# One more token tile through the DMA transpose, its plain load moved back, and a key stage opened with three tiles

## The chip, the cores and the metric

The kernel runs on one core of one Trainium2 chip. The metric is the time of one execution on the device, in microseconds (us). A profile of one execution gives its span from the first to the last instruction; the executions take some 2.0 to 2.1 us more than that. Runs are compared in rounds on the same chip, fast runs with fast runs. All results below are correct against the reference.

The engines' short names: PE is the TensorE matmul, PEld its weight load, DVE is VectorE, ACT is ScalarE, POOL is GpSimd, SP is SyncE. SP and ACT each issue loads on a hardware DMA queue of their own.

## The reference, cut to what matters

A linear-attention block and a token-mixing MLP share the input `x` (2048 tokens x 512, bf16) and are mixed by a gate. Only the keys matter here:

```python
qkv = (x @ wqkv)...                 # wqkv is 512 x 1536; the middle 512 columns give k
phi = lambda t: where(t > 0, t + 1, exp(t)) + 1e-6
pk  = phi(k)
kv  = einsum("bhsd,bhse->bhde", pk, v)   # the kernel uses x^T pk and multiplies by Wv afterwards
...                                 # normalizer, output projection, layernorm + MLP, gate
```

## The kernel before: the parts that the change and the argument touch

The tokens are cut into 16 tiles of 128. A tile's keys are four matmuls of 128x512, one for each quarter of `wk` (128 of the 512 inputs). They need the tile transposed (`xT`). Tiles 0 to 3 are loaded plainly into `xs` and transposed by TensorE with an identity; tiles 4 to 15 are transposed by DMA straight from DRAM and are loaded plainly as well, because the next matmul (`gacc`, which accumulates x^T pk) wants them untransposed.

The loads at the start, in the order in which they are issued on the queues of SP (`nc.sync`) and ACT (`nc.scalar`):

```python
load_x(nc.sync, 0, 1)
load_x(nc.scalar, 1, 1)
load_wk(nc.sync, 0)
load_x(nc.scalar, 2, 1)
load_x(nc.sync, 3, 1)
for k, q in ((1, nc.scalar), (2, nc.sync), (3, nc.scalar)):
    load_wk(q, k)
load_xT(4, 2)                 # DMA transpose of tiles 4 and 5, on SP
load_xT(6, 2)
load_x(nc.sync, 4, 4)
for t0, n in ((8, 4), (12, 4)):
    load_xT(t0, n)
    load_x(nc.sync, t0, n)
# ... wq, w1, wv, wo
```

The opening of the key stage:

```python
warm_up(6)                    # six matmuls on constants, for TensorE's clock
# ...
HEADS = 4
transpose_tile(0, False)      # four PE transposes and a copy on DVE (True: on ACT)
transpose_tile(1, True)
transpose_tile(2, False)
ln_step(0)
for k in range(2):            # first and second quarter of wk, tiles 0 to 2
    for t in range(HEADS - 1):
        k_part(t, (k,))
transpose_tile(HEADS - 1, True)
ln_step(1)
for t in range(HEADS):        # third and fourth quarter; all four for tile 3
    k_part(t, range(2 if t < HEADS - 1 else 0, ND))
    k_phi(t)
LAG = 4
for t in range(HEADS, NT):
    k_part(t, range(ND))
    k_phi(t)
    g_tile(t - LAG)           # gacc of tile t - 4
    # ... layernorm statistics of tile t - 3 on DVE
```

Below, "the first group" is the first-quarter matmuls of tiles 0 to 2, "the second group" their second-quarter matmuls, and "the third group" what begins with tile 0's third-quarter matmul.

The compiled program gives the hardware queues eight completion counters in turn. So the ninth DMA waits for the first to land before it is issued.

## Time and profile before

Before: 166.06 us (median of 3, from 165.96 to 166.17). The profiled execution:

| | |
|---|---|
| span | 164.0 us |
| PE busy | 158.9 us, 97% |
| chain that ended last | 95% PE |
| PE waits | 1.0 us in all, before 3.8 us |
| key stage (first key matmul to first `uacc`) | 5.01 to 33.14 us |

From the page of the kernel before: the span, and of part 1 busy time, share and number of instructions; of part 4 the shares of the chain of waits by engine.

```profile
span 164.0 us, 2057 instructions
PE 158.9 (97%) x771; PEld 74.1 (45%) x785; DVE 87.8 (54%) x200; ACT 58.7 (36%) x90; POOL 18.3 (11%) x37
PE 95%; DMA 2%; issue 1%; ACT 0%; DVE 0%
```

The kernel is bound by TensorE, so a few matmuls fewer ought to shorten it by their own length, as long as PE is not made to wait.

From the timeline of the kernel before, PE alone: start, length, engine, line, operation, tiles, shapes and count; in brackets how long the engine was idle before and what ended that.

```profile
2.93 0.63 PE L108 MATMUL wps<-const-bfloat16-1.0 128*128 128x512 bf16 x1
3.77 1.40 PE L194 MATMUL pt<-ident,xs 128*128 128x128 bf16 x12 [0.21 <-DMA xs<-in_A_x_dram]
5.01 1.74 PE L108 MATMUL kacc<-wk_sb,xT 128*128 128x512 bf16 x6
6.59 0.39 PE L194 MATMUL pt<-ident,xs 128*128 128x128 bf16 x4
6.81 2.11 PE L108 MATMUL kacc<-wk_sb,xT 128*128 128x512 bf16 x9
```

After the warm-up come the twelve transposes of tiles 0 to 2, the first and second group (six matmuls from 5.01 us), tile 3's four transposes (from 6.59 us) and the third group (from 6.81 us), which are the first of many matmuls without a gap. On PE the four transposes take the time from 6.59 to 6.81 us, which is 0.22 us.

From the timeline of SP's queue before (start and length of the issue, not of the transfer):

```profile
0.81 0.40 SPq L124 DMA_DIRECT2D xs<-in_A_x_dram  x1
1.27 0.43 SPq L127 DMA_DIRECT2D wk_sb<-in_A_wqkv_dram  x1
1.75 0.43 SPq L124 DMA_DIRECT2D xs<-in_A_x_dram  x1
2.23 0.44 SPq L127 DMA_DIRECT2D wk_sb<-in_A_wqkv_dram  x1
3.56 2.85 SPq L130 DMA_TRANSPOSE xT<-in_A_x_dram  x2
```

The first DMA transpose is the ninth DMA and goes out only at 3.56 us, when a completion counter is free.

### The profile page before, as it was taken

Reading aid. Unit: us, or ns where it says so; the run is one execution under the profiler, and the core shown is the slowest. Engines: PE = TensorE matmul, PEld = TensorE weight load, DVE = VectorE, ACT = ScalarE, POOL = GpSimd, SP = SyncE. Lnnn points to the kernel's source line nnn. Section 1 sums busy time; section 2 is a strip of 40 time slices with the busy share of each in tenths; the row PEclk is TensorE's granted clock in tenths of the full one; section 3 lists DMA queues with packets and bytes.
Section 4 is the critical chain, followed back from the end, with each engine's and each line's share of the span. In section 5 each row is a group of like instructions: output and inputs, shape, how many; then the busy total and the mean of one; then the engine's idle time right before and its main releaser. Section 6 shows DMA issues by size and latency. Waiting matters only on the chain.

```text
span 164.0 us, 2057 instructions
## 1 busy us (share of the span) xinstructions
PE 158.9 (97%) x771; PEld 74.1 (45%) x785; DVE 87.8 (54%) x200; ACT 58.7 (36%) x90; POOL 18.3 (11%) x37
## 2 busy tenths in 40 slices
PE   7999999999999999999999999999999999999992
PEld 2544444444544444434444444444444444444471
DVE  0599999958999999009994401256211111111131
ACT  3463386658577373212322113111122221111110
POOL 5000710200200000001055500050000000000000
PEclk9999999999999999999999999999999999999999
DMA  4999999999930005800993599932010011101001
GB/s 147 242 213 252 288 297 356 350 348 349 317 86 0 0 0 184 268 0 0 288 293 91 182 306 297 326 129 79 32 36 32 32 36 50 42 32 36 32 32 32
DMA packets 29993, 25.05 MB, mean 153 GB/s; under 512 B 7776, under 2 KB 29408, under 8 KB 29984
## 3 DMA queue, kind: packets, MB, share of 16 engines
q1 hardware_dynamic: 27968, 22.02, 45.0%
q0 software_dynamic: 1440, 2.38, 5.3%
q10 hardware_dynamic: 576, 0.52, 1.1%
q8 instruction: 6, 0.10, 0.3%
q14 instruction: 3, 0.02, 0.0%
HBM read 21.11 MB, written 2.23 MB: 142 GB/s over the span
## 4 chain that ended last, share of the span: by engine, by line
PE 95%; DMA 2%; issue 1%; ACT 0%; DVE 0%
PE uacc L108 29%; PE yps L108 29%; PE qacc L108 8%; PE gacc L108 8%; PE aps L108 8%; PE kacc L108 8%; DMA xs<-in_A_x_dram 2%; PE pt L194 1%; PE denps L108 1%; PE kvps L108 1%; PE wps L108 1%; ACT xT L198 0%; DVE ot L472 0%; PE zps L108 0%; PE pt L323 0%
## 5 line engine op out<-in xcount | busy, mean ns | idle before, releaser
L108 PE MATMUL uacc<-hs,w1c 128*128 128x512 bf16 x218 | 51.6, 379 | 0.4
L108 PE MATMUL yps<-uT,w2c 128*128 128x512 bf16 (+1 forms) x235 | 50.8, 366 | 0.2
L472 DVE SCALAR_TENSOR_TENSOR ot<-yps,c,a_sc 128x512 bf16<-128x512 f32 (+1 forms) x17 | 12.2, 719 | 46.1 <-PE yps L108 46.1
L108 PEld LDWEIGHTS <-w2c 128*128 128x128 bf16 x238 | 23.3, 98 | 25.3
L108 PEld LDWEIGHTS <-w1c 128*128 128x128 bf16 x224 | 21.6, 98 | 26.1 <-issue 0.4
L457 ACT ACTIVATE a_sc<-aps,c,gg 128x512 f32<-128x512 f32 x16 | 12.4, 778 | 46.7 <-PE aps L108 43.0
L317 ACT ACTIVATE uT<-uacc,bcol 128x512 bf16<-128x512 f32 x14 | 9.3, 687 | 27.7 <-PE uacc L108 27.7
L108 PE MATMUL qacc<-xT,wq_sb 128*128 128x512 bf16 x64 | 16.4, 379 | 0.0
L108 PE MATMUL aps<-W2sb,pqT 128*128 128x512 bf16 x62 | 16.2, 379 | 0.1
L108 PE MATMUL kacc<-wk_sb,xT 128*128 128x512 bf16 x63 | 15.9, 379 | 0.1
L108 PE MATMUL gacc<-pk,xs 128*128 128x512 bf16 x62 | 15.5, 379 | 0.1
L244 ACT ACTIVATE hs<-xs,nmr,rstd 128x512 bf16<-128x512 bf16 x16 | 12.8, 804 | 1.9 <-DVE nmr L238 1.9
L204 ACT ACTIVATE e<-qacc 128x512 bf16<-128x512 f32 x16 | 9.6, 597 | 10.1 <-PE qacc L108 10.1
L413 POOL DMA_DIRECT2D rex<-rd_dram x16 | 9.5, 603 | 23.0 <-DVE pqT L415 18.1
L204 ACT ACTIVATE e<-kacc 128x512 bf16<-128x512 f32 x16 | 9.3, 595 | 6.9 <-PE kacc L108 5.6
L208 DVE SCALAR_TENSOR_TENSOR pk<-kacc,e 128x512 bf16<-128x512 f32 x16 | 11.1, 692 | 0.6
L208 DVE SCALAR_TENSOR_TENSOR pqT<-qacc,e 128x512 bf16<-128x512 f32 x16 | 11.1, 692 | 0.6
L228 DVE BATCH_NORM_STATS2 stats<-xs 128x6 f32<-128x512 bf16 x16 | 10.9, 682 | 0.0
L205 DVE TENSOR_SCALAR e<-e 128x512 bf16<-128x512 bf16 x32 | 9.0, 281 | 3.1 <-ACT e L204 3.1
L400 DVE CUSTOM_DVE_ANT_0 junk<-xs,gw_b 128x512 bf16<-128x512 bf16 x16 | 9.8, 683 | 0.0
L108 PEld LDWEIGHTS <-xs 128*128 128x128 bf16 x64 | 6.3, 98 | 7.5
L108 PEld LDWEIGHTS <-pqT 128*128 128x128 bf16 x64 | 6.3, 98 | 7.6
(64 smaller groups left out, 73.2 us busy)
## 6 DMA issues: line engine op xcount, KB each, us to landing
w2c<-in_B_w_dram SPq DMA_DIRECT2D x4, 1792.0 KB, 8.8
w1c<-in_B_w_dram SPq DMA_DIRECT2D x2, 2048.0 KB, 15.5
w1c<-in_B_w_dram SPq DMA_DIRECT2D x3, 1024.0 KB, 12.3
rex<-rd_dram POOLq DMA_DIRECT2D x16, 128.0 KB, 2.9
out_dram<-ot SPq DMA_DIRECT2D x15, 128.0 KB, 1.7
xs<-in_A_x_dram SPq DMA_DIRECT2D x3, 512.0 KB, 5.3
wq_sb<-in_A_wqkv_dram SPq DMA_DIRECT2D x1, 512.0 KB, 6.9
wv_sb<-in_A_wqkv_dram SPq DMA_DIRECT2D x1, 512.0 KB, 10.9
```

The source lines that it names most:

```text
L108: nc.tensor.matmul(o, lhsT=lhsT, rhs=rhs, start=start, stop=stop, **kw)
L194: nc.tensor.transpose(pt[:, k * P : (k + 1) * P], xs[:, t, k * P : (k + 1) * P], ident[:])
L204: nc.scalar.activation(out=e[:], in_=acc[:], func=ACT.Exp)
L205: nc.vector.tensor_scalar(out=e[:], in0=e[:], scalar1=1.0, scalar2=PHI_EPS, op0=ALU.min, op1=ALU.add)
L208: nc.vector.scalar_tensor_tensor(out=dst, in0=acc[:], scalar=0.0, in1=e[:], op0=ALU.max, op1=ALU.add)
L228: nc.vector.bn_stats(out=stats[:], in_=xs[:, t, :])
L244: nc.scalar.activation(out=hs[:, t, :], in_=xs[:, t, :], func=ACT.Identity, scale=rstd[:, t : t + 1], bias=nmr[:, t : t + 1],)
L317: nc.scalar.activation(out=uT[:, j, :], in_=acc[:], func=ACT.Gelu_apprx_tanh, bias=bcol[:, j : j + 1])
L400: nc.vector.tensor_tensor_reduce(out=junk[:], in0=xs[:, t, :], in1=gw_b[:], scale=1.0, scalar=0.0, op0=ALU.mult, op1=ALU.add, accum_out=gp ...
L413: nc.gpsimd.dma_start(out=rex[:], in_=src.unsqueeze(1).to_broadcast([8, HEAD, SC]))
L457: nc.scalar.activation(out=a_sc[:], in_=aps[:], func=ACT.Identity, scale=gg[:, t : t + 1], bias=c2[:, t : t + 1],)
L472: nc.vector.scalar_tensor_tensor(out=ot[:, :W], in0=yps[:, :W], scalar=c1[:, t : t + 1], in1=a_sc[:, cs], op0=ALU.mult, op1=ALU.add,)
```

## The change

Its intent: save TensorE tile 3's four transposes and ACT their copy, by giving tile 3 to the DMA transpose as well; take tile 3's plain load from the crowded start, since it is then needed only by `gacc` and the statistics; and open the key stage with three tiles.

```diff
     load_x(nc.scalar, 2, 1)
-    load_x(nc.sync, 3, 1)
     for k, q in ((1, nc.scalar), (2, nc.sync), (3, nc.scalar)):
         load_wk(q, k)
-    load_xT(4, 2)
-    load_xT(6, 2)
-    load_x(nc.sync, 4, 4)
+    load_xT(3, 2)
+    load_xT(5, 3)
+    load_x(nc.sync, 3, 5)
 ...
-    HEADS = 4
+    HEADS = 3
     transpose_tile(0, False)
     transpose_tile(1, True)
     transpose_tile(2, False)
     ln_step(0)
+    ln_step(1)
     for k in range(2):
-        for t in range(HEADS - 1):
+        for t in range(HEADS):
             k_part(t, (k,))
-    transpose_tile(HEADS - 1, True)
-    ln_step(1)
     for t in range(HEADS):
-        k_part(t, range(2 if t < HEADS - 1 else 0, ND))
+        k_part(t, range(2, ND))
         k_phi(t)
 ...
-        g_tile(t - LAG)
+        if t >= LAG:
+            g_tile(t - LAG)
```

## The prediction

> **What bounds the kernel.** TensorE. The page gives PE 158.9 us of a 164.0 us span (97%); the chain that ended last is 95% PE; the view of waits lists 1.0 us for PE, all before 3.8 us. From 5.5 to 33.09 us, the end of the key stage, the chain is unbroken matmuls. DVE is nearly as full there (3.79 of 4 us in 20–24 us).
>
> **What the change removes.** Tile 3's four TensorE transposes. In the chain they stand at 6.75 us and cost 0.22 us (4 x 55 ns), all on the critical path. Also gone is a 0.60 us ACT copy at 7.01 us, off the path; DVE's phi work, which starts at 8.13 us, should move forward by about 0.2 us with the matmuls. The order of the rest hardly changes: tile 3's key matmuls come as one group of four at about 8.05 us; the first gacc group still follows tile 4.
>
> **What it adds and moves.** One more 128 KB tile through the DMA transpose: the two early transposes land about 7.66 and 8.55 us, 0.9 us apart for 256 KB, so a tile costs an estimated 0.45 us of DMA. Against that, a 128 KB load leaves the front of the SP queue, and the first transpose goes out sooner. Before, it was the ninth DMA of the two hardware queues; the program has eight completion counters, so it waited for the first load, 0.9 us on SP in the view of waits (issued at 3.56 us). Now it is the eighth and needs no wait: issue at about 2.2 us, landing (3.6 to 4.1 us on) at 6 to 7 us, needed at 8.05. Tiles 5–7: issue about 3.6, landing by about 9 us, needed at 10.65. Plain tile 3 (five-tile load, issue near 5.7, 5.3 us to land): about 11 us; needed by DVE's statistics near 13, by gacc near 15. Tiles 8–11 land no later than before (13.58), needed at 15.7. The w1 block lands at 26.7 against a need at 33.1. None should reach the chain.
>
> **The risk.** The transposes now run while the last two key weights are landing (before: issued 2.2 us, landing about 6.4–6.7 us); TensorE will want them at 6.75 and 6.97 us, 0.22 us sooner. The Trainium skill ("DMA: Bandwidth & Descriptors", section "Issuing engines are not separate DMA queues") says that all queues run on the same 16 engines and interleave. If the fourth quarter slips by over 0.3 us, PE stalls and the gain is eaten, at worst for some 0.5 us net loss. About one chance in five.
>
> **Predicted time.** 166.06 - 0.22 - a little = 165.8 us; 8 in 10: 165.4 to 166.3. Faster by over 2%: 0.01; within 2%: 0.98; slower by over 2%: 0.01.
>
> **What would show it.** Right: key matmuls contiguous from 5.5 us; key stage ends at about 32.87 us; every later stage as long as before; first DMA transpose issued near 2.2 us without a wait. Wrong: a PE wait on wk_sb or xT between 6.6 and 9 us, or on xs/pk near 13–15 us; a first transpose that still waits; DVE's last pk of the key stage (ends 31.81 us now) not moving forward, so that the last gacc group waits.
>
> **What would make it wrong.** The fourth key weight delayed by the transposes on the shared DMA engines; a transpose much slower beside plain loads; a shift of the first tile's landing, which would move the whole run.

## The result, and the profile after

The changed kernel took 166.31 us (median of 6, from 165.57 to 166.57); the kernel before, in the same rounds, 166.10 us (median of 6, from 165.96 to 166.50). The ratio is 1.0007, with a 95% interval from 0.9984 to 1.0029: the same. (Ratios here are the mean time of one kernel's fast runs over that of the other's of the same rounds, so not quite the ratio of the medians quoted.) The profiled execution took 166.53 us. All outputs are right.

From the page after, the lines of the span, of busy time, and of the chain:

```profile
span 164.3 us, 2060 instructions
PE 159.9 (97%) x781; PEld 74.0 (45%) x781; DVE 87.8 (53%) x200; ACT 58.2 (35%) x89; POOL 18.2 (11%) x37
PE 94%; DMA 3%; ACTq 1%; DVE 0%; issue 0%
```

PE's busy time is no measure of the saving. The trace of before holds ten matmul records fewer (771 against 781), although the program has four more, because some records are missing from a trace; and a 128x512 matmul at the slow clock counts for longer (0.63 us in the traces, against 0.38 at the full clock). The program itself has eight PE instructions fewer after the change: four transposes and their weight loads.

PE's timeline after:

```profile
2.93 0.63 PE L108 MATMUL wps<-const-bfloat16-1.0 128*128 128x512 bf16 x1
3.49 1.46 PE L193 MATMUL pt<-ident,xs 128*128 128x128 bf16 x12
4.75 1.39 PE L108 MATMUL kacc<-wk_sb,xT 128*128 128x512 bf16 x3
6.40 2.53 PE L108 MATMUL kacc<-wk_sb,xT 128*128 128x512 bf16 x11 [0.26 <-DMA wk_sb<-in_A_wqkv_dram]
```

The four transposes are gone, and the first tile happens to start 0.28 us sooner (3.49 against 3.77 us). But PE now waits for a quarter of `wk`, and the second group starts at 6.40 us, against 5.94 before.

SP's queue after:

```profile
0.81 0.40 SPq L124 DMA_DIRECT2D xs<-in_A_x_dram  x1
1.27 0.89 SPq L127 DMA_DIRECT2D wk_sb<-in_A_wqkv_dram  x2
2.20 4.57 SPq L130 DMA_TRANSPOSE xT<-in_A_x_dram  x2
6.81 0.58 SPq L124 DMA_DIRECT2D xs<-in_A_x_dram  x1
```

The first transpose goes out at 2.20 us without a wait, as predicted.

This looks like the risk that the prediction named: transposes that go out sooner delay the weights. The experiments do not bear it out.

### The profile page after: what moved, and what is told of

Read it like the earlier page. It is cut to its first block, busy times and chain, and to the rows that moved or that the text cites. A ratio compares the mean times of both kernels' runs of the same rounds, so it can differ in the third digit from the quotient of the medians.

```text
span 164.3 us, 2060 instructions
## 1 busy us (share of the span) xinstructions
PE 159.9 (97%) x781; PEld 74.0 (45%) x781; DVE 87.8 (53%) x200; ACT 58.2 (35%) x89; POOL 18.2 (11%) x37
## 4 chain that ended last, share of the span: by engine, by line
PE 94%; DMA 3%; ACTq 1%; DVE 0%; issue 0%
PE uacc L108 30%; PE yps L108 29%; PE gacc L108 8%; PE qacc L108 8%; PE aps L108 8%; PE kacc L108 8%; DMA wk_sb<-in_A_wqkv_dram 3%; PE denps L108 1%; PE kvps L108 1%; ACTq L124 1%; PE wps L108 1%; DVE ot L471 0%; PE zps L108 0%; PE pt L322 0%
## 5 line engine op out<-in xcount | busy, mean ns | idle before, releaser
L108 PE MATMUL kacc<-wk_sb,xT 128*128 128x512 bf16 x64 | 16.5, 389 | 0.3 <-DMA wk_sb<-in_A_wqkv_dram 0.3
L108 PEld LDWEIGHTS <-xT 128*128 128x128 bf16 x64 | 6.4, 99 | 8.2 <-issue 0.6
L268 DVE TENSOR_TENSOR zacc<-zacc,pk 128x512 f32<-128x512 f32 x14 | 9.6, 685 | 0.2
```

The lines of the kernel that those rows point to most:

```text
L108: nc.tensor.matmul(o, lhsT=lhsT, rhs=rhs, start=start, stop=stop, **kw)
L268: nc.vector.tensor_tensor(out=zacc[:], in0=first, in1=pk[:, t, :], op=ALU.add)
```

## The experiments

The theories:

- **A, contention.** The transposes, which now reach the DMA engines while the weights are landing, delay the second quarter of `wk`.
- **B, chance.** That quarter lands at scattered times in either kernel, and the two profiles drew differently.
- **C, the clock.** TensorE's clock was released late by chance (5.89 us after, 4.97 us before), which lengthened the opening.
- **D**. Everything after the start of the third group takes a fixed time. What scatters is that start, for the reasons of B and C; the change saves its 0.22 us of PE work under that scatter.

### 1 and 2. Both kernels once more, unchanged

No edit.

> The changed kernel once more, unchanged. Theory A (the DMA transposes, now on the engines from 4.75 us, hold up the second key weight quarter): it lands after 6.1 us again and PE waits for wk_sb at the second group of key matmuls; median 166.2 to 166.5 us, so no gain over before. Rival B (chance: that quarter lands anywhere between 5.6 and 6.4 us in either kernel): this profile shows a landing near 5.8 us and no wait, and the time falls to 165.7 to 165.9. Rival C (the TensorE clock was released late, 5.89 against 4.97 us, by chance): whatever the landing, the start of the third group of key matmuls follows the clock's release.

> The kernel before once more, as the control for scatter. Theory A: the second key weight quarter lands near 5.8 us and PE does not wait for it; 166.0 to 166.2 us. Rival B: landing anywhere from 5.6 to 6.4 us, with a PE wait in some profiles. Rival C: if the clock is released near 5.9 us here too, the third group of key matmuls starts later than 6.81 us and the time is up by 0.3 us or more.

Measured: after_again 166.05 us (median of 6, from 165.57 to 166.29), before_again 166.24 us (median of 5). The kernel before took 166.29 us in these rounds (median of 11, from 166.06 to 166.51). The ratio of after_again is 0.9980 (0.9964 to 0.9995), that of before_again 0.9996 (0.9983 to 1.0009). So the same changed kernel reads 0.07% slow in one set of rounds and 0.2% fast in the next.

The new profiles turn the first picture round. PE's timeline of before_again:

```profile
3.83 0.84 PE L194 MATMUL pt<-ident,xs 128*128 128x128 bf16 x12 [0.26 <-DMA xs<-in_A_x_dram]
4.74 1.00 PE L108 MATMUL kacc<-wk_sb,xT 128*128 128x512 bf16 x3
6.16 0.81 PE L108 MATMUL kacc<-wk_sb,xT 128*128 128x512 bf16 x3 [0.42 <-DMA wk_sb<-in_A_wqkv_dram]
6.81 0.39 PE L194 MATMUL pt<-ident,xs 128*128 128x128 bf16 x4
7.09 1.89 PE L108 MATMUL kacc<-wk_sb,xT 128*128 128x512 bf16 x8
```

PE's timeline of after_again:

```profile
3.64 1.26 PE L193 MATMUL pt<-ident,xs 128*128 128x128 bf16 x12
4.76 4.06 PE L108 MATMUL kacc<-wk_sb,xT 128*128 128x512 bf16 x17
```

Now it is the kernel before that waits for the second quarter (0.42 us), and the changed kernel that does not. The wait does not belong to the change.

The next table holds the four profiles side by side. A landing is the last of the sixteen completion events of a load in the trace; the clock's release is from the trace's clock records; "to the end" is from the start of the third group to the last instruction.

| us | before | before_again | after | after_again |
|---|---|---|---|---|
| tile 0 lands | 3.73 | 3.78 | 3.45 | 3.59 |
| clock at full | 4.97 | 3.52 | 5.89 | 4.16 |
| second quarter of wk lands | 5.83 | 6.12 | 6.36 | 5.58 |
| third quarter of wk lands | 6.72 | 7.04 | 6.10 | 5.16 |
| second group starts | 5.94 | 6.16 | 6.40 | 5.64 |
| third group starts | 6.81 | 7.09 | 7.04 | 6.29 |
| third group to the end | 157.18 | 157.19 | 157.27 | 157.28 |
| span | 163.99 | 164.27 | 164.31 | 163.57 |
| this execution | 166.13 | 166.32 | 166.53 | 165.70 |

Three things are to be read here. First, the third group's start, and with it the span, moves by 0.28 us within the kernel before and by 0.75 us within the changed one; the effect that is looked for is 0.22 us. Second, from the second group's start to the third's it takes 0.87 us in before (6.81 - 5.94) and 0.65 us in both profiles after: the four transposes are gone from it, 0.22 us. (In before_again it is 0.93 us, because the third quarter landed only at 7.04 us.) How much of that time another wait would have taken anyway is another matter. Where PE waited for a quarter, its matmul began 0.04 us after the landing (6.36 and 6.40 us in after, 6.12 and 6.16 us in before_again). So the third group could not have begun before about 6.76 us in before and 7.09 us in before_again, with or without the transposes: there they cost an estimated 0.05 us and nothing. The change can gain their 0.22 us at the start only because it also moves the third quarter one place up on SP's queue, where it landed at 6.10 and 5.16 us. Third, what follows the third group is fixed, but not equal: it is longer by 0.09 us after the change. That is taken up in experiments 9 to 11.

The table also weighs theory C against B. In all four profiles the second group began only 0.04 to 0.11 us after its quarter had landed; less the 0.04 us from landing to matmul, that leaves the clock and the rest of the opening at most 0.07 us. before_again has the earliest release of the clock and the latest start. In these four it was the landings that set the start.

The clock can be seen in the timelines too. Twelve transposes took 0.84 us in before_again and 1.46 us in after. The Trainium skill ("TensorE: Matmul & The Clock Gate", section "Wait — 56ns, not 53.3ns?") gives 106.7 ns from one 128-column matmul to the next while the array is cold and 55.6 ns once warm; the traces agree, with 107 ns and 55 to 56 ns between starts.

### 3. The plain load left early

```diff
     load_x(nc.scalar, 2, 1)
+    load_x(nc.sync, 3, 1)
     for k, q in ((1, nc.scalar), (2, nc.sync), (3, nc.scalar)):
 ...
-    load_x(nc.sync, 3, 5)
+    load_x(nc.sync, 4, 4)
```

> The change with one part undone: tile 3's plain load stays at its old early place, so the first DMA transpose is again the ninth DMA and waits for the first load. Theory A: its first packets come at about 5.05 us as before and not 4.75, the second key weight quarter lands near 5.8 us, PE does not wait for it, and the 0.22 us of the four transposes is gained: 165.8 to 165.9 us. Rival B: landing and time scatter as in the changed kernel, median 166.1 to 166.4.

Measured: 165.98 us (median of 6), fast runs from 165.84 to 166.50 and one slow run of 172.23 us; ratio of the fast runs 0.9982 (0.9968 to 0.9997). That is what theory A expected, but it is also what the changed kernel itself gave in the same rounds (0.9980), so it tells nothing apart. The profile fell on the slow run (granted clock 0.95) and is not used for times. But the order of events in its opening agrees with what was said above: with the transposes gone and the loads in the old order, PE waited for the third quarter, which landed at 6.66 us. PE's timeline of keep_x3:

```profile
4.87 1.68 PE L108 MATMUL kacc<-wk_sb,xT 128*128 128x512 bf16 x6
6.70 1.50 PE L108 MATMUL kacc<-wk_sb,xT 128*128 128x512 bf16 x6 [0.15 <-DMA wk_sb<-in_A_wqkv_dram]
```

### 4. The transposes held back until the second quarter has landed

```diff
+    nc.gpsimd.tensor_copy(out=xT[:, 0, 3 * P : 3 * P + 1], in_=wk_sb[:, 1, 0:1])
     load_xT(3, 2)            # must now wait for the copy, which it overwrites
```

(The loads from here on were moved, in the same order, behind the constants that POOL and DVE make.)

> The change with the DMA transposes held back until the second key weight quarter has landed (a one-column copy from that weight into the destination of the first transpose, which the transpose then overwrites). Nothing of a transpose can then delay that quarter. Theory A: it lands by 5.7 us at the latest and PE does not wait for it; PE then waits some 1.0 to 2.0 us for the xT tiles near 8 us, and the total is near 167.5. Rival B: it lands between 5.6 and 6.4 us all the same.

Measured: 167.80 us, one run, whose state is unknown. The second quarter landed at 5.61 us, with no transpose issued before 5.88 us. The waits of PE in this kernel (who waited for what; total us, times, longest):

```profile
PE kacc L108 <- DMA xT<-in_A_x_dram: 1.7, 1, 1.7
PE wps L108 <- PEq L493: 0.8, 1, 0.8
```

The landing agrees with theory A, but after_again had 5.58 us with the transposes in flight, so it does not speak for A alone. The larger sample that the later runs gave says more. Here are the landings in all profiles of fast runs, held starts of below included (those do not touch the first loads), without the two kernels that load in the order of experiments 8 and 12, and without late_T, whose transposes were held back:

| us | old order of loads (before, before_again, held_before, held_keep_x3, held2_before) | mean | new order, transposes free (after, after_again, held_after, held2_after, held2_split) | mean |
|---|---|---|---|---|
| second quarter | 5.83, 6.12, 6.14, 6.13, 5.96 | 6.04 | 6.36, 5.58, 6.06, 6.38, 5.22 | 5.92 |
| third quarter | 6.72, 7.04, 6.66, 7.05, 6.92 | 6.88 | 6.10, 5.16, 5.86, 6.19, 4.99 | 5.66 |
| fourth quarter | 6.51, 6.80, 6.90, 6.87, 6.64 | 6.74 | 6.62, 5.84, 6.38, 6.66, 5.72 | 6.24 |

Theory A is not borne out: on the mean the second quarter lands no later with the change, 5.92 against 6.04 us. But with the change it scatters more widely (5.22 to 6.38 us), and five profiles of each do not exclude a delay of some tenths of a us. Nor do they say what the transposes do alone, since the change also takes a load of 128 KB from the front; late_T, which would, is one profile. The third quarter, which moved one place up on SP's queue, lands 1.2 us sooner, and the last quarter to land comes some 0.7 us sooner (means of 6.93 and 6.24 us). The earlier issue of the transposes moves their packets by less, presumably because these still stand behind the weights on the same queue: they came first at 4.76 us after the change, against 5.20 before, for an issue at 2.20 against 3.56.

### 5 to 7. A start held until everything has landed, first try

If theory D holds, a start that no landing can touch must bare the 0.22 us. A chain of twelve DVE adds of zeros ends in the identity which the transposes need; more warm-up matmuls bridge the time.

```diff
     nc.vector.memset(Z32[:], 0.0)
+    nc.vector.memset(zacc[:], 0.0)
+    for _ in range(12):
+        nc.vector.tensor_tensor(out=zacc[:], in0=zacc[:], in1=zacc[:], op=ALU.add)
 ...
+    nc.vector.tensor_tensor(out=ident[:], in0=ident[:], in1=zacc[:, 0:P], op=ALU.add)
 ...
-    warm_up(6)
+    warm_up(22)
```

> The kernel before with its first TensorE work held back to about 9.5 us: a chain of twelve DVE adds (0.69 us each) of zeros ends in the identity that the transposes need, and 22 warm-up matmuls keep the clock up meanwhile. By then all early loads have landed and the clock is at full. Theory D (everything after the start of the third key quarter takes a fixed 157.2 us, and what scatters is only when the first loads land and when the clock is released): some 171 to 172.5 us, no PE wait for wk_sb or xT, and a scatter between executions below 0.15 us. Rival E (the later stages scatter too): a scatter of 0.3 us and more, as in the kernel before.

> The changed kernel held back in the same way. Theory D: 0.22 us below held_before (the four transposes, 4 x 55 ns) in mean and in the profile, between 0.17 and 0.30 us, since no landing can hide or eat it. Rival E (the change also costs something after the start, or its gain is not there): a difference within 0.1 us of zero.

> Held back likewise, with tile 3 by DMA transpose but its plain load left early. Theory D: the order of the loads no longer matters, so it equals held_after within 0.1 us. If instead moving the load does something for the later stages, it lies nearer to held_before.

Measured, four runs each: means of 173.54, 173.11 and 173.23 us, but scattered over 1.0 to 1.8 us (held_before from 172.68 to 174.50). No difference can be read from that: these three failed as time measurements. The profile of held_before says why. PE's timeline:

```profile
10.91 0.83 PE L198 MATMUL pt<-ident,xs 128*128 128x128 bf16 x12 [3.17 <-DVE ident L172]
11.81 2.74 PE L108 MATMUL kacc<-wk_sb,xT 128*128 128x512 bf16 x6
14.34 0.63 PE L198 MATMUL pt<-ident,xs 128*128 128x128 bf16 x4
14.77 2.48 PE L108 MATMUL kacc<-wk_sb,xT 128*128 128x512 bf16 x9
```

The warm-up ended too soon; PE was idle for 3.17 us, and the clock fell back at 11.66 us, in the midst of the first key matmuls, which then started 0.43 us apart and no longer 0.22. The idle time was 2.37 us in the profile of held_after, and there it did not fall back. It is a fault of the experiment, and at the same time a measurement of what the clock (C) alone can cost: over 1 us (spans of 172.1 and 170.6 us). The record of all twelve executions agrees: the six from 173.5 us up have a granted clock of 0.988 to 0.990, the six below 172.9 us one of 0.997 to 1.000. The six undisturbed ones, two of each kernel, average 172.76 us (held_before), 172.67 (held_after) and 172.55 (held_keep_x3); that is too few to read, but it is the order that experiments 9 to 11 show.

### 8. A try at a better version: the second quarter first

```diff
-    load_x(nc.scalar, 2, 1)
-    for k, q in ((1, nc.scalar), (2, nc.sync), (3, nc.scalar)):
-        load_wk(q, k)
+    load_wk(nc.scalar, 1)
+    load_wk(nc.sync, 2)
+    load_x(nc.scalar, 2, 1)
+    load_wk(nc.scalar, 3)
 ...
+    # first three quarters of tiles 0 and 1, then tile 2's transposes,
+    # then the fourth quarter of tiles 0 and 1, then all of tile 2
```

> A try to beat both: the changed kernel with the second key weight quarter loaded ahead of tile 2 on its queue, and the key work of tiles 0 and 1 ahead of tile 2's transposes. If the landing of that quarter (5.6 to 6.4 us so far) is what holds the start, it now lands near 4.5 us, PE has no wait for it, the twelve opening key matmuls end by about 7.8 us (8.34 and 7.59 us in the two profiles of the changed kernel), and the time is 165.5 to 165.8 us with less scatter. If the landings as a whole only trade places (tile 2 or the fourth quarter then being the late one), the time stays at 166.0 to 166.3 us with PE waits for those instead.

Measured: 166.51 us (median of 6); ratio 1.0022 (1.0003 to 1.0042), so slower by a hair. The second quarter landed at 4.43 us as meant. But the clock was released only at 6.36 us in the profiled execution, and the new order made tile 2's matmuls wait for their copy on DVE. From the timeline of this kernel:

```profile
7.22 0.42 DVE L200 COPY xT<-pt 128x512 bf16<-128x512 bf16 x1 [1.16 <-PE pt L194]
7.70 2.27 PEld L108 LDWEIGHTS <-xT 128*128 128x128 bf16 x12 [0.58 <-DVE xT L200]
```

### 9 to 11. The held start again, with the clock kept up

As in 5 and 6, with `warm_up(30)`. The third kernel of this set takes up the 0.09 us at the end. The change merges two loads into one, so the program has one hardware DMA fewer, and the last store signals another of the eight counters. held2_split parts the load again, in the same place:

```diff
-    load_x(nc.sync, 3, 5)
+    load_x(nc.sync, 3, 1)
+    load_x(nc.sync, 4, 4)
```

> The held start again with 30 warm-up matmuls in place of 22, so that TensorE is idle for about 2 us at most before its first transpose and keeps its clock (with 22 the clock fell back in one of the three profiles, at 11.66 us, and that alone made the scatter of 1.8 us). Theory D: first transpose at about 10.91 us, 22 PE groups without a wait, span near 170.7 us and executions near 172.8 us, scattering by no more than 0.2 us. If the executions still scatter by 0.5 us and more, something after the start scatters too.

> The changed kernel, held likewise. Theory D with the tail: the four transposes save 0.22 us at the start, but with one DMA fewer the last store's completion counter is asked for one step earlier in the closing row of counter checks, which costs 0.06 to 0.09 us after it (in all profiles so far the stretch from the first gacc matmul to the end is 154.25 us where the load was merged and 154.16 where not). So 0.13 us below held2_before, between 0.08 and 0.18. Without the tail's part it would be 0.22; if the change gains nothing, zero.

> held2_after with the merged load of tiles 3 to 7 split into tile 3 and tiles 4 to 7, in the same place behind the transposes: the number of DMAs is that of the kernel before again. If the count of DMAs sets the tail, the stretch from the first gacc matmul to the end is 154.16 us and the time 0.22 us below held2_before (0.09 below held2_after). If the tail comes from something else, it equals held2_after.

Measured, four runs each:

| | runs, us | mean | against held2_before |
|---|---|---|---|
| held2_before | 172.72, 172.87, 172.74, 172.82 | 172.79 | |
| held2_after | 172.69, 172.60, 172.60, 172.62 | 172.63 | -0.16 |
| held2_split | 172.44, 172.45, 172.52, 172.50 | 172.48 | -0.31 |

The kernel before scattered over 0.78 us in these rounds (165.71 to 166.49); held, the scatter is 0.15 us and less, and the runs of the three kernels no longer overlap. PE's timeline of held2_before:

```profile
10.91 0.83 PE L198 MATMUL pt<-ident,xs 128*128 128x128 bf16 x12 [1.22 <-DVE ident L172]
11.81 1.65 PE L108 MATMUL kacc<-wk_sb,xT 128*128 128x512 bf16 x6
13.30 0.39 PE L198 MATMUL pt<-ident,xs 128*128 128x128 bf16 x4
13.52 3.19 PE L108 MATMUL kacc<-wk_sb,xT 128*128 128x512 bf16 x13
16.54 0.38 PE L108 MATMUL gacc<-pk,xs 128*128 128x512 bf16 x1
```

PE's timeline of held2_after:

```profile
10.91 0.83 PE L197 MATMUL pt<-ident,xs 128*128 128x128 bf16 x12 [1.57 <-DVE ident L171]
11.82 4.67 PE L108 MATMUL kacc<-wk_sb,xT 128*128 128x512 bf16 x19
16.32 0.59 PE L108 MATMUL gacc<-pk,xs 128*128 128x512 bf16 x2
```

PE's timeline of held2_split:

```profile
10.91 0.83 PE L198 MATMUL pt<-ident,xs 128*128 128x128 bf16 x12 [1.78 <-DVE ident L172]
11.82 4.67 PE L108 MATMUL kacc<-wk_sb,xT 128*128 128x512 bf16 x19
16.32 0.59 PE L108 MATMUL gacc<-pk,xs 128*128 128x512 bf16 x2
```

All three start at 10.91 us, and the first `gacc` comes at 16.54 or at 16.32 us: 0.22 us, the four transposes. From there to the start of the last matmul it is 150.65 us in all three. To the last instruction it is 154.16, 154.25 and 154.16 us. So the 0.09 us lie behind the last matmul, and parting the load takes them away again. (In the other unheld and held profiles of fast runs, and in late_T, it is the same: 154.25 to 154.26 us with the merged load and 154.16 to 154.17 us without, whatever else was changed.) Where they are shows in the closing row of counter checks on SP, read from the trace of the first two profiles (start of each check in us, and the hardware counter that it asks for):

```
before  161.813 (103)  161.877 (104)  162.858 (105, last store)  162.917 (106)  162.979 (107)  163.038 (108)  163.099 (109)
after   162.042 (103)  163.115 (104, last store)  163.177 (105)  163.236 (106)  163.298 (107)  163.357 (108)  163.419 (109)
```

The last store's counter is asked for one step earlier in the row, and five checks of 0.06 us follow it, not four. From the check that waits for the last store to the closing drain it takes 0.31 us before and 0.37 us after: 0.06 of the 0.09 us. The rest is in the last store itself: from its issue to its landing it took 1.53 us in before and 1.56 us in after, and so in all fourteen profiles, 1.53 to 1.54 us where it signals counter 105 and 1.56 to 1.57 us where it signals 104. Why was not found. By spans, the net gain of the change with a held start is 0.22 - 0.09 = 0.13 us and that of the split version 0.22 us; by executions they came to 0.16 and 0.31 us. The difference lies between executions and spans: the three profiled executions took 2.02, 2.12 and 1.96 us more than their spans, and why was not found.

### 12. A second try at a better version

The loads of experiment 8, tile 2's transposes ahead of the third quarter, tile 1's copy on DVE and tile 2's on ACT, and the load parted as in held2_split.

```diff
     transpose_tile(0, False)
-    transpose_tile(1, True)
-    transpose_tile(2, False)
+    transpose_tile(1, False)
 ...
+    for t in range(2):
+        k_part(t, (0, 1))
+    transpose_tile(2, True)
+    # third quarter of tiles 0 and 1, then the fourth, then all of tile 2
```

> A try to beat both: the loads of wk1_first (second weight quarter ahead of tile 2), but tile 2's transposes before the third quarter's matmuls, tile 1's copy on DVE and tile 2's on ACT, so that no PE group waits for a copy as the last one did for 0.47 us; the load split as in held2_split. The twelve opening key matmuls should end 0.2 us sooner than the changed kernel's at the same clock release, and no wait should be over 0.2 us: 165.6 to 165.9 us, against 166.2 for before. If the clock's release dominates (it came between 3.5 and 6.4 us in the profiles so far), the mean is near 165.9 with the same scatter.

Measured: 166.01 us (median of 6, from 165.73 to 166.21), against 166.25 for before (median of 11, from 165.71 to 166.49); ratio 0.9988 (0.9971 to 1.0005). That is not clear of the scatter. The waits of PE:

```profile
PE wps L108 <- PEq L497: 0.8, 1, 0.8
PE pt L195 <- DMA xs<-in_A_x_dram: 0.4, 1, 0.4
```

The second quarter landed at 4.09 us, and it was now tile 2, put behind it, that came late: it landed at 6.24 us. The landings traded places. In these two tries, what the order of a queue took from one load it gave to another; the opening needs seven loads of 128 KB, whatever their order.

## Why the prediction was right or wrong, point by point

- **The class, and the size.** Right as a class: nothing near 2%. The estimate was 165.8 us, 0.26 us below before. The first six runs had a median of 166.31 us, against a stated range up to 166.3, and a ratio of 1.0007; the next six had 166.05 us and 0.9980. All twelve runs of the changed kernel average 166.12 us, and the 17 of the kernel before in the same rounds 166.25 us (22 with those of before_again, with the same mean). That agrees with a gain of about 0.13 us, but the scatter of these runs leaves it uncertain by some 0.2 us, so they do not prove one.
- **"Cost 0.22 us (4 x 55 ns), all on the critical path".** Right about the PE work: with a held start the first `gacc` comes at 16.32 and not 16.54 us. "All on the critical path" was not so, even in the profile that it was read from. The chain shows who came last, and not who came just before: in before the third quarter landed at 6.72 us and would have let the third group begin at about 6.76 us instead of 6.81, so only some 0.05 us of the four transposes were exposed. In before_again the third quarter landed at 7.04 us, the third group followed at 7.09 us, and none of them was. What opens the rest of the 0.22 us is the part of the change that the prediction counted only for the transposes' sake: the plain load of tile 3 that leaves the queue ahead of the third quarter, which then lands at 5.66 and not 6.88 us on the mean. How much of the 0.22 us the unheld kernel gains was not shown.
- **"Every later stage as long as before".** Right up to the last matmul (150.65 us from the first `gacc` in all three held kernels) and wrong behind it: one DMA fewer moved the last store's counter, for 0.09 us. This is the term of the sum that was left out: with a held start, 0.22 should have been 0.13.
- **"From 5.5 to 33.09 us ... the chain is unbroken matmuls", and therefore "key matmuls contiguous from 5.5 us", "key stage ends at about 32.87 us".** This was the weak step. It took one execution's opening for the kernel's opening. The key stage ended at 33.37 us in the first profile after and at 32.62 us in the second; before, at 33.14 and 33.42 us. What sets it in these four are the landings of the second and third quarters. The release of the clock, which came anywhere from 3.52 to 6.48 us in the fourteen profiles, can add to it where the landings are early, as in experiment 8. The stated range of -0.4 to +0.5 us was wide enough, but for other reasons than the ones given.
- **The risk.** It was named as the fourth quarter delayed by the transposes, at one chance in five. The first profile after shows a wait for `wk_sb`, but for the second quarter, and the kernel before shows the same wait in its second profile. The five landings in either order average 5.92 us with the change and 6.04 us without. The fourth quarter, which the risk was about, lands sooner on the mean, 6.24 against 6.74 us. So the risk as stated did not come about, although the first profile looked much like it. What the prediction took from the skill, that the queues share the engines and interleave, agrees with the trace as far as interleaving goes: in before the eight first loads landed by turns, one of ACT's queue and one of SP's (the last four at 5.83, 6.05, 6.51 and 6.72 us). That they share the engines was not measured apart.
- **The first transpose.** Its issue at 2.2 us without a wait was right (2.20 us). Its landing "at 6 to 7 us" was not: 7.50 and 6.74 us. On the mean of the five profiles of each order, an issue about 1.4 us sooner brought the first transpose in 0.64 us sooner (7.19 against 7.83 us).
- **The other landings.** "By about 9 us" for tiles 5 to 7 was 8.86 us, "about 11 us" for the plain tile 3 was 11.80 us, and tiles 8 to 11 came at 13.72 us, against 13.60 us before. PE waited for none of them.
- **DVE's last pk** of the key stage, which was to move forward from 31.81 us, ended at 31.99 us in the first profile after, because that opening was late; the last `gacc` group did not wait for it.

What stays open: why the landings scatter. Packets of loads that usually take 46 ns took up to 0.83 us in before and 0.94 us in after, in the first 9 us; what holds them was not measured. No version is shown to beat both kernels in the unheld form. By the held runs the changed kernel with its load parted should be the best of them (0.22 us rather than 0.13), but it was not run unheld, where the scatter of about 0.8 us would drown it. The held runs also measure only what PE and the tail do once all loads have landed; what the new order of loads is worth in the unheld opening was not measured apart.

## What to carry to other kernels

Before a saving of 0.2 us is argued from two profiles, see how far two profiles of the same kernel differ; here the start alone moved by up to 0.75 us, and a wait that seemed to belong to the change turned up in the old kernel. To measure a small saving behind a scattering start, hold the start in both kernels until loads and clock have settled, and keep TensorE busy meanwhile, so that its clock does not fall back; that brought the scatter from 0.8 us down to 0.15 us and bared the sum's terms one by one. Before a piece of work is called critical because it stands in the chain, look what else its successor waits for and when that came; here a load that landed 0.09 us before the third group began would have taken most of the saving. And count what a change does to the number of DMAs: which completion counter the last store gets was worth 0.09 us at the end here.

## What the Trainium skill lacked or had wrong

- "TensorE: Matmul & The Clock Gate", section "What's actually happening", puts the clock's window at 3413 ns, running freely, and says "That's why the transition point varies ±500ns". The window fits: the full clock was held for whole multiples of 3.413 us in the profiles (two in held_before before it fell back, 47 in before), and the slow clock between for one. The spread does not: with the first warm-up matmul at 0.84 to 0.85 us, the release came between 3.52 and 6.48 us in fourteen profiles, a spread of 2.96 us.
- The same page's section has the clock fall back after an idle window of about 3.4 us. In held_before it fell back after 3.17 us of idle time followed by 0.75 us of work. Counted in steps of 3.413 us from the release at 4.84 us, the window that ended at 11.66 us had begun at 8.25 us: TensorE worked in its last 0.75 us, and the clock fell back all the same. After 2.37 us (held_after) it did not, but there the idle time also lay across the border of two such windows (9.89 us).
- "Advanced Engine Details and Errata", section "X-Bar Transpose (TRN2)", says that "TRN2 transpose DMAs are as fast as regular DMAs". Here a transpose moved in packets of 256 bytes of 18 ns each (median), which is 72 ns for a KB, where plain loads took 46 ns for a packet of 1 KB. These are times of packets; the rate of a whole transpose beside a whole load was not compared.
- No page was found that says what the closing row of completion checks costs: about 0.06 us for each check that stands behind the one of the last store.
